# Routing operands moved from SBUF to PSUM in a one-core attention, expert and MLP kernel

## The chip, the cores and the metric

The kernel runs on one core of a Trainium2 chip. The metric is the device time of one execution in microseconds (us). The kernel before takes 499.25 us, the median of three runs (498.87 to 499.83). Besides these there is one profiled execution, from which all the rows below come.

## The reference

Three stages follow one another: attention over 2 batches and 8 heads with rotary positions, a top-1 mixture of 8 experts over 1152 tokens, and a dense MLP with a softplus-tanh gate. What matters here is the middle one: each token goes to the expert of its largest logit, so the kernel has to count the tokens of each expert and find a place for every token before any expert work can start.

```python
q_rot, k_rot = rotate(q), rotate(k)                  # 2 x 8 heads, 576 rows, 64 wide
scores = scale * q_rot @ k_rot.T
attn = exp(scores - max) / (sum + 1e-9);  x = attn @ v       # -> [1152, 512]
logits = x @ w_gate + modality_bias[modality_id]      # 8 experts
e_idx = argmax(logits);  gate_w = softmax(logits)[e_idx]
for e in range(8):
    mask = e_idx == e
    out[mask] = gate_w[mask] * (relu(x[mask] @ w1[e]) @ w2[e])
h = out @ w_in                                        # 512 -> 2048
g = h * tanh(softplus(h));  return g @ w_out
```

## The kernel before

The tokens are handled as two halves of 576, one for each batch. Products are made in float32 accuracy from pairs: each operand is split into a high part (`hi`, written by ScalarE) and a low part (`lo` = value minus `hi`, written by VectorE or GpSimd), and TensorE multiplies hi with hi, hi with lo and lo with hi.

Attention runs head by head. The order of its instructions on each engine is worked out ahead of time by a planner (`Plan`), which holds a modelled duration for each operation and always issues the one that can start first. While it works on the second half, the routing of half 0 is one of the planner's streams. The line `plan.op("rt_cp", "dve", 0.9, ...)` tells it how long the first block of VectorE operations behind the counting matmul takes, and `rest()` adds the following ones.

`routing(b)` is the routing of one half. From the logits it makes a one-hot table `oh`, lets TensorE count it by two matmuls into a PSUM bank `ps` (named `counts` for half 0 and `mm` for half 1), and makes from it each token's row number (`pos`, then `row` as int32, L405). GpSimd scatters the tokens' rows to DRAM with five indirect DMAs. Then comes a table of tiles: from the counts per expert (`ce`, `n1`, `qi`) the expert and first row of each tile of 304 tokens (`te`, `tm`, `tbl`). The helper `near` lays a small tile into a corner of a PSUM bank (`cur["rtile"]`, named `rt` or `sc` in the profile) in place of SBUF. `nx` is the number of tiles beyond the first two. `merge_extra` joins the leftover tiles of both halves into one list for a loop that runs only if there are any; its first line (L535) compares `iotat` (0, 1, 2, ...) with `nxs[0]`, half 0's count. With `mm`, `md` and `ei` it makes the list, and `nxi` is the sum of both counts.

The routing of half 1 runs after attention, beside the first expert tile. A loop at the end of the kernel goes through its steps, and after each VectorE step lets the generator of expert work (`gen0`) issue some TensorE work:

```python
for i, y in enumerate(chain(route(1), merge_extra(nx))):
    if i in P["dl"]:
        dec_load(len(wr))
    if y[0] == "dve":
        pump(P["rq"][(i > 9) + (i > 20)])
```

So VectorE's queue alternates between routing operations and the `hl` operations (L731) of the expert tile, which give TensorE the low part of its second product. An expert tile takes eight chunks of weights, `whi` (ScalarE, L609) and `wlo` (L614, GpSimd but for two chunks of the first tile). TensorE reads `hh`, `hl`, `whi` and `wlo` in its order (L706). Each engine takes its instructions strictly in the order issued. There are four expert tiles, (0, 0) to (1, 1). In between, VectorE decodes the weights of the last stage (`rt`, `wc`: L1318, L1323, L1328), a step after a set number of TensorE steps. The last stage is a loop over 2 groups and 16 blocks, whose costliest VectorE operation is a reciprocal (L1524).

Of the kernel before, what the change touches and what calls it, by code (L numbers as in the profile page):

```python
# [10 lines left out]
F32 = mybir.dt.float32  # L11
F32R = mybir.dt.float32r
I32 = mybir.dt.int32
AF = mybir.ActivationFunctionType
ALU = mybir.AluOpType
# [3 lines left out]
B, H, S, D = 2, 8, 576, 64  # L19
# [6 lines left out]
T = 304  # L26
# [186 lines left out]
def moe_kernel(ctx: ExitStack, tc: tile.TileContext, aps, out):  # L213
    nc = tc.nc
# [8 lines left out]
    rp = xctx.enter_context(tc.tile_pool(name="rp", bufs=1, side="right"))  # L223
# [16 lines left out]
    iotat = kp.tile([128, NS[1]], F32, name="iotat")  # L240
# [71 lines left out]
    scat, nxs, tes, tms = ([], []), [], [], []  # L312
    early = []

    def routing(b, bank):
        t = lambda sh, nm, dt=F32: rp.tile(sh, dt, tag=nm, name=f"{nm}{b}")
        side = True
        room = [0]

        def near(sh, nm):  # L320


            if not side:
                return t(sh, nm)
            n = 1
            for x in sh[1:]:
                n *= x
            o = room[0]
            room[0] += n
            v = cur["rtile"][0:sh[0], o:o + n]  # L330
            if len(sh) == 3:
                v = v.rearrange("p (a b) -> p a b", b=sh[2])
            return v

        V = nc.vector
# [4 lines left out]
            out=lg, in_=heads(X[b])[:, :, :, D:XW].rearrange("p j h e -> p j e h"),  # L340
# [15 lines left out]
            out=val, in0=lg, scalar=0.0, in1=iota8[:, 0:1, :].to_broadcast(sh),  # L356
            op0=ALU.is_ge, op1=ALU.mult,
# [9 lines left out]
        n = NE * 5  # L367
        yield "pe", 0.43, True
        ps = bank()
# [5 lines left out]
        def scan():  # L375
# [8 lines left out]
            out=base[:, 1:], data0=ps[:, 0:n], data1=zero[:, :n],  # L384
# [3 lines left out]
        V.tensor_tensor(out=pz, in0=ps[:, n:2 * n], in1=base[:, 0:n], op=ALU.add)  # L388
        V.tensor_copy(cnt[:, 0:n], ps[:, 0:n])
        V.tensor_tensor(out=pz, in0=pz, in1=ohf, op=ALU.mult)  # L390
        pos = t([128, 5], "pos") if b == 0 else near([128, 5], "pos")
        V.tensor_reduce(
            out=pos, in_=pz.rearrange("p (e j) -> p j e", j=5), axis=AX.X, op=ALU.add
        )
        sm8 = t([128, 5], "sm8")
        yield "dve", 0.12, True
        V.tensor_reduce(out=sm8, in_=ex, axis=AX.X, op=ALU.add)
# [1 line left out]
        nc.scalar.activation(out=sm8, in_=sm8, func=AF.Copy, bias=1e-9)  # L399
        yield "dve", 0.12, True  # L400
        V.reciprocal(out=X[b][:, :, XC + 1], in_=sm8)
        row = t([128, 5], "row", I32)
        s1, o1 = (-1.0, T + S - 1.0) if b == 0 else (1.0, float(T + S))
        yield "dve", 0.12, True
        V.tensor_scalar(out=row, in0=pos, scalar1=s1, scalar2=o1, op0=ALU.mult, op1=ALU.add)  # L405

        def scatters():
            for j, (_, qn) in enumerate(QT):
# [15 lines left out]
        else:  # L424
            cur["scatters"] = scatters()
            yield "mark", 0.0, False
            side = False
# [5 lines left out]
        n0 = t([1, NE], "n1")  # L433
# [5 lines left out]
            out=n1, in0=ce, scalar=float(T), in1=n0, op0=ALU.is_gt, op1=ALU.add  # L439
        )  # L440
        if side:
# [5 lines left out]
            out=qi, data0=n1, data1=zero[0:1, :NE], initial=0.0, op0=ALU.add, op1=ALU.add  # L447
# [7 lines left out]
            out=st, in0=s0, scalar=float(-T), in1=base[0:1, 0:n:5], op0=ALU.mult, op1=ALU.add  # L455
        )
        ns = NS[b]
        nx = t([1, 1], f"nx{b}")
        yield "dve", 0.12, True
        V.tensor_scalar(  # L460
            out=nx, in0=qi[:, NE - 1:NE], scalar1=-2.0, scalar2=None, op0=ALU.add
        )
        tv = iotat[0:1, 0:ns]
        if b:
# [3 lines left out]
                out=tv[:, 0:2], in0=iotat[0:1, 0:2], scalar1=nx, scalar2=None, op0=ALU.add  # L468
# [3 lines left out]
                out=tv[:, 2:ns], in0=iotat[0:1, 2:ns], scalar1=nxs[0], scalar2=-2.0,  # L472
                op0=ALU.subtract, op1=ALU.add,
# [7 lines left out]
            out=lt, in0=qi[:, None, :].to_broadcast(s8),  # L481
            in1=tv[:, :, None].to_broadcast(s8), op=ALU.is_le,
        )
        te = t([1, ns, 2], f"te{b}")
        tm = near([1, ns, 2], "tm") if side else te
        yield "dve", 0.12, True
        V.tensor_reduce(out=tm[:, :, 0], in_=lt, axis=AX.X, op=ALU.add)
        e8 = near([1, ns], "e8")
# [4 lines left out]
            out=lt, in0=iota8[0:1, 0:1, :].to_broadcast(s8),  # L493
            in1=e8[:, :, None].to_broadcast(s8), op=ALU.is_equal,
# [8 lines left out]
            out=cs, in0=tv, scalar=float(T), in1=cs, op0=ALU.mult, op1=ALU.add  # L503
# [9 lines left out]
            op0=ALU.max, op1=ALU.min,  # L513
# [2 lines left out]
        V.tensor_scalar(  # L516
            out=tm[:, :, 0], in0=tm[:, :, 0], scalar1=float(NE - 1), scalar2=None, op0=ALU.min
        )
        if side:
            yield "dve", 0.12, True  # L520
            V.tensor_copy(te, tm)
        tes.append(te)
        tms.append(tm)
        tbl[b] = ti = const.tile([1, 2, 2], I32, name=f"tbl{b}")
# [3 lines left out]
    def merge_extra(nx):  # L528

        V = nc.vector  # L530
        n0, n1 = NS[0] - 2, NS[1] - 2
        sh = [1, n0, 2]
        m = rp.tile([1, n0], F32, tag="mm", name="mm")
        yield "dve", 0.12, True
        V.tensor_scalar(  # L535
            out=m, in0=iotat[0:1, 0:n0], scalar1=nxs[0], scalar2=None, op0=ALU.is_lt
        )
        d = rp.tile(sh, F32, tag="md", name="md")
        yield "dve", 0.12, True
        V.tensor_tensor(out=d, in0=tes[0][:, 2:], in1=tms[1][:, 2:2 + n0], op=ALU.subtract)  # L540
        yield "dve", 0.12, True
        V.tensor_tensor(out=d, in0=d, in1=m[:, :, None].to_broadcast(sh), op=ALU.mult)
        yield "dve", 0.12, True
        V.tensor_tensor(
            out=tes[1][:, 2:2 + n0], in0=tms[1][:, 2:2 + n0], in1=d, op=ALU.add
        )
        ei = const.tile([1, n1, 2], I32, name="ei")
        yield "dve", 0.12, True
        V.tensor_copy(ei, tes[1][:, 2:])
        yield "dve", 0.12, True  # L550
        V.tensor_tensor(out=nx, in0=nxs[0], in1=nxs[1], op=ALU.add)
        cur["ei"] = ei

    def tile_regs(row):
# [676 lines left out]
    def hook(plan, bank):  # L1231

        r0 = route(0)
        cur["rbank"] = lambda: bank("counts")

        def until_mark():
            for y in r0:
                if y[0] == "mark":
                    return
                yield y  # L1240

        def mark(name):
            return lambda t: plan.done.update({name: ("dve", t)})

        def start():
            plan.add(until_pe(r0), plan.now, end=mark("rt"), gate=cur["spare"])

        def rest():
            next(r0)
            plan.add(until_mark(), plan.now + 0.8, end=mark("rt_row"))  # L1250

        def scatter():
            plan.add(cur["scatters"], plan.now, low=("pool",), end=mark("rt_sc"))

        def table():
            plan.add(r0, plan.now, end=mark("rt_end"))

        def weights():
            tile_rows(0)
            plan.add(until_pe(gen0), plan.now + 2.2, low=LOW)  # L1260

        z = 10.0 * H
        plan.op(
            "route", "sp", 0.0, z, start,
            deps=[("norm", n, f) for n in range(H) for f in range(2)],
        )
        plan.op("rt_mm", "pe", 0.43, z, lambda: next(r0), deps=["rt"], take=[("ring", "rt")])
        plan.op("rt_cp", "dve", 0.9, z, rest, deps=["rt_mm"], give=[("ring", "rt")])
        plan.op("scatter", "sp", 0.0, z, scatter, deps=["rt_row"])
        plan.op("table", "sp", 0.0, z, table, deps=["rt_row", ("plo", B * H - 1)])  # L1270
        plan.op(
            "rows", "sp", 2.2, z, weights,
            deps=["rt_end", "rt_sc", ("stack", B * H - 1), ("vload", B * H - 1)],
        )
# [430 lines left out]
```

## Time and profile before

| What | Value |
|---|---|
| Median of three runs | 499.25 us (498.87 to 499.83) |
| The profiled execution's own time | 501.34 us |
| Its span, first to last instruction | 499.5 us |
| TensorE busy, share of the span | 470.3 us, 94% |
| VectorE busy, share of the span | 399.8 us, 80% |
| GpSimd busy, share of the span | 361.1 us, 72% |
| ScalarE busy, share of the span | 332.8 us, 67% |
| Mean granted TensorE clock | 0.997 |

Engines are named as in the profile: PE is TensorE, DVE VectorE, ACT ScalarE, POOL GpSimd, SP the engine that only issues transfers. A row of the timeline gives start and duration in us, then engine, line, operation, written tile, read tiles and their shapes; behind it, in brackets, how long the engine had been idle and what it had waited for. A duration on VectorE can hold a wait that no bracket shows, since the instruction has already begun. The clock is given as a share of 2.4 GHz, so that 0.5 is 1.2 GHz.

### The profile page before, as it was taken

How to read it: one execution, taken by the hardware profiler on the slowest of the kernel's cores; microseconds unless marked ns; L12 is line 12 of the kernel's file. 1: busy time of each engine (PE TensorE's matmuls, PEld its weight loads, DVE VectorE, ACT ScalarE, POOL GpSimd, SP SyncE). 2: the span in 40 equal slices, each digit the busy share in tenths (PEclk: the TensorE clock that was granted, in tenths of full speed). 3: DMA queues.
4: the chain of work that ended last, by engine and by line, in shares of the span. 5: the costliest groups of instructions: out<-in, count | busy, mean ns of one | idle time of the engine just before them, and what ended most of it. 6: DMA issues, size and time to landing. Idle time of an engine off the chain costs nothing.

```text
span 499.5 us, 8770 instructions
## 1 busy us (share of the span) xinstructions
PE 470.3 (94%) x2996; PEld 430.3 (86%) x2996; DVE 399.8 (80%) x614; ACT 332.8 (67%) x751; POOL 361.1 (72%) x363
## 2 busy tenths in 40 slices
PE   1699999998999898999999999999999999999995
PEld 1589999997998797998999998898989887888894
DVE  5789889899798587663777779999999959777773
ACT  2488788777778754464564478666656778777663
POOL 3899989999870554675957457778678668977654
PEclk9999999999999998999999999999999999999999
DMA  6589985788564497786975340020200001100002
GB/s 218 137 200 240 227 232 149 183 214 193 150 175 142 160 394 283 259 309 249 326 283 211 113 141 0 2 85 1 85 1 1 1 1 42 42 22 1 1 0 86
DMA packets 24131, 69.41 MB, mean 139 GB/s; under 512 B 5522, under 2 KB 9810, under 8 KB 22034
## 3 DMA queue, kind: packets, MB, share of 16 engines
q1 hardware_dynamic: 21794, 63.16, 41.2%
q0 software_dynamic: 1456, 5.03, 2.5%
q10 hardware_dynamic: 832, 0.61, 0.4%
q8 instruction: 25, 0.41, 0.3%
q14 instruction: 24, 0.20, 0.1%
HBM read 49.08 MB, written 6.44 MB: 111 GB/s over the span
## 4 chain that ended last, share of the span: by engine, by line
PE 40%; DVE 8%; issue 3%; POOL 1%; ACT 1%; POOLq 0%; DVEq 0%; ACTq 0%
PE h L1498 15%; PE o L1559 14%; PE mm L706 11%; DVE ta L1524 6%; DVE wc L1328 1%; DVE ta L1525 1%; PE mm L672 0%; POOL out_dram L1569 0%; DVE wc L1318 0%; DVE wc L1323 0%; POOLq L1701 0%; POOL g L1542 0%; DVE idi L1645 0%; ACT ot L1565 0%; DVE yl L1436 0%
## 5 line engine op out<-in xcount | busy, mean ns | idle before, releaser
L1524 DVE RECIPROCAL ta<-ta 128x320 f32<-128x320 f32 (+1 forms) x64 | 124.6, 1947 | 21.4 <-ACT ta L1517 21.4
L1472 POOL TENSOR_TENSOR w2l<-wc,w2h 128x512 fp32r<-128x512 f32 x64 | 89.4, 1418 | 15.3 <-DVE yl L1436 8.1
L1559 PE MATMUL o<-w2h,g 128*128 128x512 f32 x288 | 97.8, 395 | 0.1
L1542 POOL TENSOR_TENSOR g<-ta,g 128x320 fp32r<-128x320 f32 (+1 forms) x63 | 52.9, 845 | 27.9 <-ACT g L1536 21.2
L969 PE MATMUL sc<-sk,sq 128*128 128x288 f32 (+1 forms) x320 | 58.3, 314 | 15.5 <-ACT sk L901 10.1
L1498 PE MATMUL h<-yl,w2h 128*128 128x320 f32 (+2 forms) x204 | 66.9, 328 | 0.1
L1498 PE MATMUL h<-yh,w2h 128*128 128x320 f32 (+2 forms) x204 | 66.9, 328 | 0.0
L1498 PE MATMUL h<-yh,w2l 128*128 128x320 f32 (+2 forms) x204 | 66.8, 328 | 0.0
L1559 PEld LDWEIGHTS o<-w2h,g 128*128 128x128 f32 x288 | 53.9, 188 | 12.2 <-POOL g L1542 1.0
L990 ACT ACTIVATE pexp<-sc,nm 128x576 f32<-128x576 f32 x72 | 53.3, 741 | 16.3 <-DVE nm L979 11.5
L1023 ACT ACTIVATE ph<-pt 128x512 fp32r<-128x512 f32 (+2 forms) x112 | 54.6, 509 | 12.5 <-PE pt L1003 12.0
L979 DVE TENSOR_REDUCE nm<-sc 128x1 f32<-128x576 f32 x72 | 53.4, 751 | 10.8 <-PE sc L969 7.3
L969 PEld LDWEIGHTS sc<-sk,sq 128*128 128x128 f32 (+1 forms) x320 | 46.4, 190 | 17.5 <-ACT sk L901 10.1
L1003 PE MATMUL pt<-ident,pexp 128*128 128x128 f32 (+1 forms) x360 | 54.9, 278 | 2.8 <-DVE pl L1029 1.7
L1559 PE MATMUL o<-w2l,g 128*128 128x512 f32 x144 | 56.8, 394 | 0.0
L1029 DVE TENSOR_TENSOR pl<-pt,ph 128x512 fp32r<-128x512 f32 (+1 forms) x80 | 48.9, 628 | 2.9 <-ACT ph L1023 2.4
L1044 PE MATMUL av<-ph,vhl 128*128 128x256 f32 (+1 forms) x160 | 50.8, 333 | 0.3 <-ACT avt L1053 0.2
L1003 PEld LDWEIGHTS pt<-ident,pexp 128*128 128x128 f32 (+1 forms) x360 | 42.1, 138 | 6.0 <-issue 2.1
L1536 ACT ACTIVATE g<-ta 128x320 fp32r<-128x320 f32 (+1 forms) x64 | 27.9, 435 | 22.5 <-DVE ta L1525 22.2
L1513 ACT ACTIVATE ta<-h 128x320 f32<-128x320 f32 (+1 forms) x64 | 25.6, 400 | 25.4 <-PE h L1498 25.3
L1498 PEld LDWEIGHTS h<-yl,w2h 128*128 128x128 f32 x204 | 38.3, 188 | 4.1 <-DVE yl L1436 0.4
L1498 PEld LDWEIGHTS h<-yh,w2h 128*128 128x128 f32 x204 | 38.3, 188 | 3.9 <-DVE ta L1525 0.2
(447 smaller groups left out, 1222.2 us busy)
## 6 DMA issues: line engine op xcount, KB each, us to landing
wr<-in_wio_dram SPq DMA_DIRECT2D x16, 1024.0 KB, 6.1
wc<-in_w_dram SPq DMA_DIRECT2D x26, 512.0 KB, 5.1
xs<-in_qk_dram SPq DMA_DIRECT2D x15, 576.0 KB, 5.3
sk<-ab SPq DMA_DIRECT2D x30, 288.0 KB, 4.1
sq<-ab SPq DMA_DIRECT2D x30, 144.0 KB, 2.7
vraw<-in_v_dram SPq DMA_DIRECT2D x16, 160.0 KB, 3.9
scratch<-zero SPq DMA_DIRECT2D x12, 108.8 KB, 4.5
xrow(0, 0)_2304<-scratch SPq DMA_DIRECT2D x2, 290.0 KB, 3.0
```

Of the source, the lines that this page charges most:

```text
L706: nc.tensor.matmul(ps[:, :T], lhsT=w, rhs=m, start=(n == 0), stop=(n == 3 * len(pairs) - 1))
L969: nc.tensor.matmul(t[:m, hf, :NC2], lhsT=sq[:, c:c + m], rhs=sk[:, z, hf * NC2:(hf + 1) * NC2], start=(z == 0), stop=(z == 1),)
L979: nc.vector.tensor_reduce(out=nm[n, j], in_=sc[n, j][:, :, :NC2], axis=AX.XY, op=ALU.max, negate=True)
L990: nc.scalar.activation(out=pe, in_=sc.pop((n, j))[:, :, :NC2], func=AF.Exp, bias=nm.pop((n, j)), accum_out=st[n, hf][:, i:i + 1],)
L1003: nc.tensor.transpose(out=t[:kn, o:o + 128], in_=pexp[n, j][:, k0:k0 + kn], identity=ident)
L1023: nc.scalar.activation(out=block(ph, n, hf, kts, slice(0, kn)), in_=psum(n, hf, kts, kn), func=AF.Copy)
L1044: nc.tensor.matmul(av[n, hf][:, :u.nq], lhsT=vhl[n][:, kt].rearrange("p a d -> p (a d)"), rhs=src[:, kt, u.at:u.at + u.nq], start=(kt == 0 ...
L1472: nc.gpsimd.tensor_tensor(out=lo[:, cs], in0=w[:, cs], in1=hi[:, cs].bitcast(F32), op=ALU.subtract)
L1498: nc.tensor.matmul(ps[:, :w], lhsT=wt[:, c], rhs=m[y][:, c], start=(n == 0), stop=(n == 11))
L1524: nc.vector.reciprocal(out=ta, in_=ta)
L1542: eng.tensor_tensor(out=gt[q][1][:, o:o + w], in0=tas.pop((q, i))[:, :w], in1=gt[q][0][:, o:o + w].bitcast(F32), op=ALU.subtract,)
L1559: nc.tensor.matmul(acc[g, t], lhsT=a[:, s], rhs=b, start=(f == 0 and z == 0), stop=(f == FC2 - 1 and z == 2),)
```

## The change

Three things are changed. The row numbers' sum `pos` goes into the counting matmul's own PSUM bank, and `row` is made from it at once, a few operations earlier than before (both halves). In `merge_extra` ScalarE first copies half 0's count from SBUF to PSUM (`first`), and the comparison becomes a TENSOR_TENSOR of `iotat` with that, written to PSUM. The merged list of half 1 is worked on in PSUM (`tm`), without the copy to `te` in SBUF. Two modelled durations of the planner are raised by 0.2.

```diff
-        pos = t([128, 5], "pos") if b == 0 else near([128, 5], "pos")
+        pos = ps[:, 3 * n:3 * n + 5]
         V.tensor_reduce(
             out=pos, in_=pz.rearrange("p (e j) -> p j e", j=5), axis=AX.X, op=ALU.add
         )
+        row = t([128, 5], "row", I32)
+        s1, o1 = (-1.0, T + S - 1.0) if b == 0 else (1.0, float(T + S))
+        V.tensor_scalar(out=row, in0=pos, scalar1=s1, scalar2=o1, op0=ALU.mult, op1=ALU.add)
...
         V.reciprocal(out=X[b][:, :, XC + 1], in_=sm8)
-        row = t([128, 5], "row", I32)
-        s1, o1 = (-1.0, T + S - 1.0) if b == 0 else (1.0, float(T + S))
-        yield "dve", 0.12, True
-        V.tensor_scalar(out=row, in0=pos, scalar1=s1, scalar2=o1, op0=ALU.mult, op1=ALU.add)
...
-        te = t([1, ns, 2], f"te{b}")
-        tm = near([1, ns, 2], "tm") if side else te
+        tm = te = near([1, ns, 2], "tm") if side else t([1, ns, 2], f"te{b}")
...
-        if side:
-            yield "dve", 0.12, True
-            V.tensor_copy(te, tm)
...
-        m = rp.tile([1, n0], F32, tag="mm", name="mm")
-        yield "dve", 0.12, True
-        V.tensor_scalar(
-            out=m, in0=iotat[0:1, 0:n0], scalar1=nxs[0], scalar2=None, op0=ALU.is_lt
+        o = cur["rtile"][0:1, 440:441 + n0]
+        first, m = o[:, n0:], o[:, 0:n0]
+        yield "act", 0.13, True
+        nc.scalar.activation(out=first, in_=nxs[0], func=AF.Copy)
+        yield "dve", 0.12, True
+        V.tensor_tensor(
+            out=m, in0=iotat[0:1, 0:n0], in1=first.to_broadcast([1, n0]), op=ALU.is_lt
         )
         d = rp.tile(sh, F32, tag="md", name="md")
+        t0 = tms[1][:, 2:2 + n0]
         yield "dve", 0.12, True
-        V.tensor_tensor(out=d, in0=tes[0][:, 2:], in1=tms[1][:, 2:2 + n0], op=ALU.subtract)
+        V.tensor_tensor(out=d, in0=tes[0][:, 2:], in1=t0, op=ALU.subtract)
...
-        V.tensor_tensor(
-            out=tes[1][:, 2:2 + n0], in0=tms[1][:, 2:2 + n0], in1=d, op=ALU.add
-        )
+        V.tensor_tensor(out=t0, in0=t0, in1=d, op=ALU.add)
...
-        V.tensor_copy(ei, tes[1][:, 2:])
+        V.tensor_copy(ei, tms[1][:, 2:])
         yield "dve", 0.12, True
-        V.tensor_tensor(out=nx, in0=nxs[0], in1=nxs[1], op=ALU.add)
+        V.tensor_tensor(out=nx, in0=first, in1=nxs[1], op=ALU.add)
...
-            plan.add(until_mark(), plan.now + 0.8, end=mark("rt_row"))
+            plan.add(until_mark(), plan.now + 1.0, end=mark("rt_row"))
...
-        plan.op("rt_cp", "dve", 0.9, z, rest, deps=["rt_mm"], give=[("ring", "rt")])
+        plan.op("rt_cp", "dve", 1.1, z, rest, deps=["rt_mm"], give=[("ring", "rt")])
```

VectorE's queue at the end of half 1's routing, before the change:

```order
L521 COPY te_2723<-rt_2545 1x36
L526 CAST tbl_2765<-rt_2545 1x4
L535 TENSOR_SCALAR mm<-iotat,nx_2116 1x8
L731 SCALAR_TENSOR_TENSOR hl(0, 0)_2576<-mm_2755,hh(0, 0)_2575 128x304
L540 TENSOR_TENSOR md<-te_2133,rt_2545 1x16
L542 TENSOR_TENSOR md<-md,mm 1x16
L544 TENSOR_TENSOR te_2723<-rt_2545,md 1x16
L549 CAST ei<-te_2723 1x32
L551 TENSOR_TENSOR nxi<-nx_2116,nx_2708 1x1
L731 SCALAR_TENSOR_TENSOR hl(0, 0)_2576<-mm_2779,hh(0, 0)_2575 128x304
```

The same place after the change (line numbers shift by a few; `rt` is the PSUM corner):

```order
L521 CAST tbl_2758<-rt_2544 1x4
L533 TENSOR_TENSOR rt_2544<-iotat,rt_2544 1x8
L539 TENSOR_TENSOR md<-te_2155,rt_2544 1x16
L541 TENSOR_TENSOR md<-md,rt_2544 1x16
L728 SCALAR_TENSOR_TENSOR hl(0, 0)_2575<-mm_2754,hh(0, 0)_2574 128x304
L543 TENSOR_TENSOR rt_2544<-rt_2544,md 1x16
L546 CAST ei<-rt_2544 1x32
L548 TENSOR_TENSOR nxi<-rt_2544,nx_2705 1x1
L728 SCALAR_TENSOR_TENSOR hl(0, 0)_2575<-mm_2781,hh(0, 0)_2574 128x304
```

The copy to `te` is gone, the comparison reads and writes `rt`, and two small operations stand ahead of the seventh `hl` that stood behind it.

ScalarE's queue there after the change; its new first-count copy is the second row:

```order
L606 ACTIVATE whi(0, 0)_5_2748<-wc_2537 128x1024
L531 ACTIVATE rt_2544<-nx_2124 1x1
L726 ACTIVATE hh(0, 0)_2574<-mm_2754 128x304
L726 ACTIVATE hh(0, 0)_2574<-mm_2781 128x304
L606 ACTIVATE whi(0, 0)_6_2798<-wc_2532 128x1024
```

Everything else in these rows stands as it did; the copy lies between the split of chunk 5 and the `hh` that the seventh `hl` reads.

VectorE's queue behind the counting matmul of half 0, inside attention, before the change:

```order
L392 TENSOR_REDUCE pos_1652<-counts 128x5
L397 TENSOR_REDUCE sm_1654<-ex_1510 128x5
L1029 TENSOR_TENSOR pl_1_1616<-pt_1_0_1603,ph_1_1615 128x512
L401 RECIPROCAL X_80<-sm_1654 128x5
L979 TENSOR_REDUCE nm_2_1687<-sc_111 128x1
L405 TENSOR_SCALAR row_1686<-pos_1652 128x5
L1084 TENSOR_TENSOR X_81<-xo_0_1636,rs_0_1479 128x3x72
L979 TENSOR_REDUCE nm_0_1702<-sc_110 128x1
L1068 RECIPROCAL rs_1_1618<-rs_1_1618 128x2
L1084 TENSOR_TENSOR X_81<-xo_1_1696,rs_1_1592 128x2x72
L1029 TENSOR_TENSOR pl_1_1616<-pt_1_2_1690,ph_1_1615 128x512
```

And after the change:

```order
L392 TENSOR_REDUCE counts<-counts 128x5
L397 TENSOR_SCALAR row_1653<-counts 128x5
L400 TENSOR_REDUCE sm_1655<-ex_1510 128x5
L1026 TENSOR_TENSOR pl_1_1616<-pt_1_0_1603,ph_1_1615 128x512
L404 RECIPROCAL X_80<-sm_1655 128x5
L976 TENSOR_REDUCE nm_2_1688<-sc_111 128x1
L1081 TENSOR_TENSOR X_81<-xo_0_1636,rs_0_1479 128x3x72
L976 TENSOR_REDUCE nm_0_1704<-sc_110 128x1
L1026 TENSOR_TENSOR pl_1_1616<-pt_1_2_1690,ph_1_1615 128x512
L1065 RECIPROCAL rs_1_1618<-rs_1_1618 128x2
L1081 TENSOR_TENSOR X_81<-xo_1_1695,rs_1_1592 128x2x72
```

The operation that makes `row` reads PSUM and stands four places earlier, and from here to the end of half 0's tile table the planner places a number of attention operations of all engines otherwise.

## Rows read from the trace of the kernel before

**Rows 1.** The chain of waits: start, duration, what; two long pieces.

```profile
235.59 20.28 PE mm L706 x144
257.95 33.60 PE mm L706 x240
```

**Rows 2.** Busy time by window: length, engines (instructions), PE clock, DMA share, GB/s.

```profile
100.00:120.00 20.00, 18.36 (x147) 17.59 (x147) 19.08 (x47) 14.86 (x40) 18.93 (x20) 1.00 0.80 211
...
188.00:190.00 2.00, 0.87 (x7) 0.61 (x5) 2.00 (x1) 1.46 (x3) 2.00 (x2) 1.00 1.06 440
190.00:192.00 2.00, 0.80 (x4) 0.54 (x4) 1.90 (x9) 0.00 (x0) 0.32 (x1) 1.00 0.99 411
192.00:194.00 2.00, 2.00 (x10) 2.00 (x11) 1.90 (x4) 1.37 (x2) 0.07 (x1) 0.59 0.96 373
194.00:196.00 2.00, 2.00 (x10) 2.00 (x10) 1.32 (x2) 0.00 (x0) 2.00 (x1) 0.55 0.35 135
```

**Rows 3.** TensorE's waits: for what, us in total, times, longest.

```profile
PE mm L706 <- DVE hl(0, 0)_2576 L731: 2.3, 2, 1.9
PE pt L1003 <- DVE pl L1029: 1.7, 3, 0.9
```

**Rows 4.** Timeline, VectorE and then GpSimd, 185 to 191 us.

```profile
186.24 0.18 DVE L521 COPY te<-rt 1x36 f32<-1x36 f32 x1
186.42 3.93 DVE L535 TENSOR_SCALAR mm<-iotat,nx 1x8 f32<-1x8 f32 x1
190.27 0.45 DVE L731 SCALAR_TENSOR_TENSOR hl(0, 0)_2576<-mm,hh(0, 0)_2575 128x304 fp32r<-128x304 f32 x1
...
185.59 2.42 POOL L614 TENSOR_TENSOR wlo(0, 0)_5_2751<-wc,whi(0, 0)_5_2749 128x1024 fp32r<-128x1024 f32 x1
187.97 2.35 POOL L614 TENSOR_TENSOR wlo(0, 0)_6_2803<-wc,whi(0, 0)_6_2801 128x1024 fp32r<-128x1024 f32 x1
```

**Rows 5.** Timeline of VectorE and GpSimd around 114 us.

```profile
113.84 1.69 DVE L405 TENSOR_SCALAR row<-pos 128x5 int32<-128x5 f32 x1
115.44 0.37 DVE L1084 TENSOR_TENSOR X<-xo,rs 128x216 f32<-128x216 f32 x1
...
112.84 2.66 POOL L912 TENSOR_TENSOR xs<-xs,tabs 128x1152 f32<-128x1152 f32 x1
```

**Rows 6.** Timeline of TensorE, 186 to 196 us, four of its matmuls.

```profile
186.05 0.30 PE L706 MATMUL mm<-hh(0, 0)_2575,whi(0, 0)_4_2697 128*128 128x304 f32 x1
...
188.56 0.30 PE L706 MATMUL mm<-hh(0, 0)_2575,whi(0, 0)_4_2697 128*128 128x304 f32 x1
190.78 0.41 PE L706 MATMUL mm<-hl(0, 0)_2576,whi(0, 0)_4_2697 128*128 128x304 f32 x1 [1.91 <-DVE hl(0, 0)_2576 L731]
...
195.91 0.30 PE L706 MATMUL mm<-hh(0, 0)_2575,whi(0, 0)_5_2749 128*128 128x304 f32 x1
```

**Rows 7.** Timeline of VectorE, GpSimd and ScalarE, 172 to 177 us.

```profile
173.95 0.22 DVE L365 TENSOR_TENSOR oh<-iota,rt 128x40 f32<-128x40 f32 x1
...
172.65 2.36 POOL L614 TENSOR_TENSOR wlo(0, 0)_2_2584<-wraw(0, 0)_2_2456,whi(0, 0)_2_2582 128x1024 fp32r<-128x1024 f32 x1 [3.36 <-ACT whi(0, 0)_2_2582 L609]
...
176.23 0.21 ACT L399 ACTIVATE sm<-sm 128x5 f32<-128x5 f32 x1 [2.70 <-DVE sm L397]
```

**Rows 8.** Timeline of TensorE, 115 to 118 us, the two rows with a wait.

```profile
115.95 0.38 PE L1003 MATMUL pt<-ident,pexp 128*64 128x128 f32 x2 [0.84 <-DVE X L1084]
...
117.49 0.84 PE L1003 MATMUL pt<-ident,pexp 128*128 128x128 f32 x6 [0.62 <-DVE pl L1029]
```

**Rows 9.** Timeline of VectorE at 182 us.

```profile
182.56 0.40 DVE L467 TENSOR_SCALAR tv<-iotat,nx 1x2 f32<-1x2 f32 x1
```

**Rows 10.** Timeline of SyncE and ScalarE for the first weight chunk of tile (0, 0).

```profile
154.93 0.34 SPq L602 DMA_DIRECT2D wraw(0, 0)_0_2332<-in_w_dram  x1
...
163.07 1.06 ACT L609 ACTIVATE whi(0, 0)_0_2345<-wraw(0, 0)_0_2332 128x1024 fp32r<-128x1024 f32 x1
```

**Rows 11.** DMA issues: KB each, median us from issue to landing.

```profile
wraw(0, 0)_0_2332<-in_w_dram SPq DMA_DIRECT2D x1, 512.0 KB, 4.4
```

## The prediction, made before the changed kernel was run

> **What bounds the kernel now.** I read the chain of waits first. From 235.6 us it runs through TensorE's L706 without a break, the two longest pieces among them 20 and 34 us long [rows 1], and goes on with TensorE and VectorE by turns to the end. So what TensorE loses before 235 us is lost at the end, unless another engine takes it back. The busy time by window shows where it loses: 1.64 us in the 20 us in which half 0's routing lies, and 1.13 and 1.20 us in the 4 us at the end of half 1's routing, with the clock at 0.59 and 0.55 in the 4 us behind that [rows 2]. TensorE's waits name the releasers: `hl` (L731) with 2.3 us in two waits, `pl` (L1029) with 1.7 us in three [rows 3]. The timeline of VectorE then shows what made them late. At 186.42 us L535, a TENSOR_SCALAR on eight numbers, takes 3.93 us; the copy ahead of it, on 36 numbers, takes 0.18 [rows 4]. GpSimd's two weight splits stand beside it without a gap, the second from 187.97 to 190.32 us, and L535 ends at 190.35 [rows 4]. Inside attention it is the same in small: L405 (`row`) takes 1.69 us and ends at 115.53, and GpSimd's product L912 ends at 115.50 [rows 5]. Both read SBUF and write SBUF. The copy at 186.24, PSUM to SBUF, ran beside the same split without delay [rows 4].
>
> **Half 1: the comparison.** L535 stands ahead of the seventh `hl` on VectorE, which therefore starts at 190.27 [rows 4], and TensorE, which wanted it after the matmul at 188.56, goes on at 190.78 [rows 6]. What this costs is read from the starts of the matmuls. From 186.05 to 188.56 there are 18 steps in 2.51 us, or 0.139 us a step. From 188.56 to 195.91 there are 21 steps in 7.35 us, where 21 x 0.139 = 2.93 would do [rows 6]. The loss is 4.42 us. It holds both waits (2.3 us, [rows 3]), the stretch at 0.59 and 0.55 of the clock, where 4 us x (1 - 0.57) = 1.7 us are lost [rows 2], and some 0.4 us of filling up again behind the waits.
>
> The new comparison is a TENSOR_TENSOR with `iotat` from SBUF, the count from PSUM, the result in PSUM. The trace has its like: L365 compares `iota` from SBUF with `rt` from PSUM and takes 0.22 us at 173.95, beside a GpSimd split that runs from 172.65 to 175.01 [rows 7]. I take 0.2 us for L533; from above it is bounded by L535's 3.93. The other operations of the list read one operand from SBUF and one from PSUM in the same way. Behind the new comparison the seventh and eighth `hl` come at some 187 us, and TensorE wants the seventh only behind 188.56. So the stall goes whole, and with it the 1.9 us wait that stands ahead of the slow clock: minus 4.4 us. What would be late next is `wlo` of chunk 6, which ends at 190.32 [rows 4]. TensorE then reaches chunk 5 at 186.05 + 24 x 0.139 = 189.4 us and chunk 6 not before 192.7 us, so it isn't.
>
> The added wait is that of L533 on ScalarE's copy of the count. Behind L533 on VectorE are two list operations and the seventh `hl`, and TensorE waits for that. The copy is a small ScalarE operation like L399 (0.21 us, [rows 7]), and reads a number that half 0's routing left long before; it stands behind the split of chunk 5, which must be over before GpSimd's own part of that chunk starts at 185.59 [rows 4]. VectorE gets to L533 at 186.3 or so. I cost it at nothing; if that cover were gone, every microsecond past some 188 us would come back to TensorE. The removed copy to `te` (0.18 us, [rows 4]) and its place in the loop, which issued two matmuls' worth of TensorE work, change the order of TensorE's work by nothing but where a register load stands. `row` of half 1 moves forward in the queue, but the scatters behind it also need the reciprocal's gate, which stays where it was.
>
> **Half 0: the row numbers.** L405's 1.69 us become some 0.2 us, since it now reads PSUM as the copy at 186.24 does [rows 4]: 1.5 us of VectorE time. Right behind it L1084 came at 115.44 [rows 5], for which TensorE had waited 0.84 us, and then 0.62 us for `pl` behind that [rows 8]. With VectorE 1.5 us earlier both waits go, which is 1.46 us at most. The other end is worked out from what else moves: the planner sets up to 40 us of attention in another order, and in the old one a misplaced `pl` costs up to 0.9 us [rows 3]; two such new waits would leave 1.46 - 2 x 0.9 = -0.3, a loss of 0.3 us. VectorE is 19.08 of 20 us busy there [rows 2] and a new order has no reason to be better or worse, so I stay near the row with the two waits and take minus 1.0 us. The two raised durations cost nothing by themselves; they only make the planner's order.
>
> **The sum.** 4.4 + 1.0 = 5.4 us off the profiled execution's own 501.34 us, 1.84 us of which lie outside its span of 499.5, gives 495.9 us. The median of the runs shown is 499.25, 2.1 us below the profiled one, and the same 5.4 us off it gives **493.8 us**. From 196 us to the last stage everything is set off by TensorE's progress, VectorE's decoding too, so I let the gain go through to the end.
>
> The Trainium skill, page "SBUF — State Buffer", section "Who interferes with whom", says that GpSimd's only pair of SBUF ports is VectorE's second pair, that it is held as an exclusive lock for a whole instruction, and that `copy`, `cast` and `tensor_scalar` from SBUF to SBUF, or an operation with two inputs in SBUF, are the ones that take it. By that rule the trace agrees: L535 and L405 both end 0.03 us behind a GpSimd operation [rows 4, 5]. The rule would leave the sum as it is, but it also speaks against the change, for the two `tv` operations ahead of the list stay TENSOR_SCALARs in SBUF; what that would do is the second rival.
>
> **Rivals.**
> *Half 1 alone pays.* The new order of attention eats what L405 gives back. For it: VectorE has little room there, and the waits of [rows 3] show that one late operation is enough. Against it: the two waits of [rows 8] stand right behind L405. Half 0 then comes to between +0.3 and -0.5, and the time is 499.25 - 4.4 + 0 = about 494.9, from 494.3 to 495.2.
> *The stall only moves.* The `tv` operations (L467 and the next) stay as they were. Before, the first ran at 182.56 in 0.40 us [rows 9], 3.0 us ahead of the first split at 185.59 [rows 4]. If they came later than that they would be held as L535 was, to the end of the second split, and TensorE with them: nothing is won in half 1, and 499.25 - 1.0 = 498.2. Against it: in the new queue they stand no later, behind the same `hl` and the same weight split. By the Trainium skill's page named above the same follows.
> *Other work takes a part back.* With TensorE 4 us further on, a weight chunk or a split comes late somewhere, or the clock falls in another place; the price of one such fall is the 1.7 us of [rows 2]. That makes 493.8 + 1.7 = 495.5, up to 497. Against it: the transfers' share falls to 0.35 at 194 us [rows 2], so they have room.
> *Slower: the tile table comes late.* Half 0's table is placed later by a few operations among attention's. SyncE needs it for the rows and issues the first weight chunk of tile (0, 0) behind it, at 154.93 us [rows 10]; it lands some 4.4 us later [rows 11], at 159.4, and ScalarE reads it at 163.07 [rows 10]. That leaves 3.7 us. From there on each microsecond of delay reaches the first expert tile, and to end above 500.3 the table would have to come 3.7 + 5.4 + 1.0 = 10 us late. A few operations of 0.7 us don't make that.
>
> **Chances and range.** About 0.2%, or 1.0 us, is what a measurement of this kernel can tell from no change. I give 0.60 to the forecast (493.8; by itself 492.8 to 494.4, the lower end if other waits of [rows 3] go too), 0.20 to half 1 alone (494.9), 0.12 to a part given back (495.5), 0.05 to a stall that moves (498.2, within reach of no change) and 0.03 to the late table. Faster by over 0.2% are the first three, and a little of the fourth: 0.92. Within: 0.05. Slower: 0.03. The range that should hold the time 8 times in 10 goes from 492.6, where half 0's two waits go whole and 0.8 us of the other waits of [rows 3] with them, to 496.4, where half of the loss behind the slow clock and all of half 0's gain are given back: 494.9 + 1.5.
>
> **What would show it.** In the changed profile the comparison, now L533, should take some 0.2 us, TensorE should go through chunks 4 and 5 of tile (0, 0) at 0.139 us a step without a wait for `hl`, and the clock should stay at 1.00 between 186 and 196 us. `row` of half 0 should take 0.2 us, and TensorE's busy time in the 20 us from 100 should rise from 18.36 towards 19.8. The prediction is wrong if a TENSOR_SCALAR of `tv` takes 2 us or more, if TensorE waits as long for something else in that tile, or if its first matmul of tile (1, 0), at 235.59 before, comes less than 4 us earlier.

## The result and the profile after

The changed kernel takes 493.63 us, the median of four runs (492.69 to 494.61); the kernel before, run beside it, takes 499.06 us (497.56 to 499.83). The ratio is 0.9895, with a 95% interval from 0.9865 to 0.9925. The profiled execution of after took 493.69 us with a span of 491.9 us, that of before 501.34 and 499.5. So the two traces differ by 7.6 us where the medians differ by 5.4: the profiled execution of before was 2.1 us above its median. Distances to before's trace below are therefore a little too large, and the medians say how large the effect is. Four profiles of the experiments lie off their medians as well: `cmp_early` by 2.2 and `cost_13` by 1.6 us above, `cmp_nx_back` by 1.2 and `half0_only` by 0.9 us below.

The chain of waits of after, beside [rows 1] (start, duration, what):

```profile
228.39 20.29 PE mm L703 x144
250.76 33.62 PE mm L703 x240
```

The same two pieces with the same lengths, 7.20 us earlier. From the first of them to the end of the span it is 263.5 us, and 263.9 before: what was won ahead of tile (1, 0) went through to the end.

To see where it was won, both traces are read from one common matmul, the first of attention that waits for `mx` (L347), to the first expert matmul of tile (0, 0) and on to the first of tile (1, 0). TensorE of after, three rows of its timeline:

```profile
100.10 0.40 PE L966 MATMUL sc<-sk,sq 128*128 128x288 f32 x1 [0.19 <-DVE mx L347]
...
168.36 0.41 PE L703 MATMUL mm<-xh(0, 0)_2503,whi(0, 0)_0_2368 128*128 128x304 f32 x1
...
228.39 0.38 PE L703 MATMUL mm<-xh(1, 0)_3275,whi(1, 0)_0_3302 128*128 128x304 f32 x1 [0.30 <-PEq L1407]
```

And of before, where the third row is the start in [rows 1]:

```profile
100.69 0.53 PE L969 MATMUL sc<-sk,sq 128*128 128x288 f32 x2 [0.18 <-DVE mx L347]
...
171.09 0.41 PE L706 MATMUL mm<-xh(0, 0)_2504,whi(0, 0)_0_2345 128*128 128x304 f32 x1
```

The stretch with half 0's routing in it went from 171.09 - 100.69 = 70.40 us to 68.26 (2.14 less), the stretch with half 1's from 235.59 - 171.09 = 64.50 to 60.03 (4.47 less). The other 0.59 us lie ahead of the common matmul, where nothing was changed. These two stretches are used for all the experiments.

**Half 1.** VectorE and then GpSimd of after, where [rows 4] stood:

```profile
183.23 0.15 DVE L521 CAST tbl<-rt 1x4 int32<-1x4 f32 x1
183.61 0.16 DVE L533 TENSOR_TENSOR rt<-iotat,rt 1x8 f32<-1x8 f32 x1 [0.23 <-issue]
183.80 0.16 DVE L539 TENSOR_TENSOR md<-te,rt 1x16 f32<-1x16 f32 x1
183.99 0.16 DVE L541 TENSOR_TENSOR md<-md,rt 1x16 f32<-1x16 f32 x1
184.52 0.47 DVE L728 SCALAR_TENSOR_TENSOR hl(0, 0)_2575<-mm,hh(0, 0)_2574 128x304 fp32r<-128x304 f32 x1 [0.36 <-ACT hh(0, 0)_2574 L726]
...
183.00 2.40 POOL L611 TENSOR_TENSOR wlo(0, 0)_5_2750<-wc,whi(0, 0)_5_2748 128x1024 fp32r<-128x1024 f32 x1
185.82 2.41 POOL L611 TENSOR_TENSOR wlo(0, 0)_6_2800<-wc,whi(0, 0)_6_2798 128x1024 fp32r<-128x1024 f32 x1 [0.42 <-ACT whi(0, 0)_6_2798 L606]
```

The comparison takes 0.16 us in the middle of `wlo` of chunk 5, and the seventh `hl` waits for nothing but its own `hh`. TensorE, for [rows 6]:

```profile
186.09 0.30 PE L703 MATMUL mm<-hh(0, 0)_2574,wlo(0, 0)_4_2699 128*128 128x304 f32 x1
...
189.84 0.31 PE L703 MATMUL mm<-hh(0, 0)_2574,wlo(0, 0)_5_2750 128*128 128x304 f32 x1
189.99 2.24 PE L669 MATMUL mm<-ident,xrow(0, 1)_2643 128*128 128x128 f32 x12
192.16 0.41 PE L703 MATMUL mm<-hh(0, 0)_2574,whi(0, 0)_6_2798 128*128 128x304 f32 x1
```

Between the first two rows lie 27 steps in 3.75 us, 0.139 us each, and no row in between has a wait.

**Half 0.** VectorE and TensorE of after, for [rows 5, 8], and by window for [rows 2]:

```profile
111.77 0.16 DVE L397 TENSOR_SCALAR row<-counts 128x5 int32<-128x5 f32 x1
...
113.28 0.38 DVE L1081 TENSOR_TENSOR X<-xo,rs 128x216 f32<-128x216 f32 x1
...
115.02 0.79 PE L966 MATMUL sc<-sk,sq 128*128 128x288 f32 x4 [0.28 <-ACT pexp L987]
...
146.09 0.89 PE L1071 MATMUL xo<-mov,avt 128*128 128x72 f32 x6 [0.63 <-DVE pl L1026]
148.96 0.27 PE L1000 MATMUL pt<-ident,pexp 128*64 128x128 f32 x1 [0.95 <-DVE tbl L521]
```

```profile
100.00:120.00 20.00, 19.62 (x158) 19.25 (x159) 19.08 (x50) 16.02 (x44) 18.68 (x23) 1.00 0.74 194
...
190.00:194.00 4.00, 4.00 (x27) 3.11 (x25) 2.75 (x7) 3.06 (x6) 1.57 (x2) 1.00 0.92 336
192.00:196.00 4.00, 4.00 (x29) 3.95 (x29) 3.71 (x7) 1.71 (x4) 2.28 (x1) 1.00 0.97 359
```

`row` takes 0.16 us, the two waits at 115 and 117 us are gone, TensorE is busy 19.62 of the 20 us for 18.36, and the granted clock stays at 1.00 behind 190 us. But 30 us later two waits of 0.63 and 0.95 us stand in attention, where before has 0.15 us (at 148.90) and 0.89 us (at 151.70): 0.54 us of TensorE's gain are lost there.

### The profile page after: what moved, and what is told of

Same layout as the page of the kernel before. It is cut to its first block, busy times and chain, and to the rows that moved or that the text cites. A ratio compares the mean times of both kernels' runs of the same rounds, so it can differ in the third digit from the quotient of the medians.

```text
span 491.9 us, 8773 instructions
## 1 busy us (share of the span) xinstructions
PE 465.8 (95%) x2996; PEld 428.4 (87%) x2996; DVE 392.8 (80%) x613; ACT 333.6 (68%) x752; POOL 361.1 (73%) x363
## 4 chain that ended last, share of the span: by engine, by line
PE 51%; POOL 0%; issue 0%; ACT 0%; POOLq 0%; DVE 0%
PE h L1495 20%; PE o L1556 20%; PE mm L703 11%; PE mm L669 0%; POOL out_dram L1566 0%; POOLq L1698 0%; ACT ot L1562 0%; DVE yl L1433 0%; ACT yh L1431 0%; ACT Y L753 0%; POOL spacer L1573 0%; POOLq L1566 0%
## 5 line engine op out<-in xcount | busy, mean ns | idle before, releaser
L1469 POOL TENSOR_TENSOR w2l<-wc,w2h 128x512 fp32r<-128x512 f32 x64 | 90.4, 1433 | 16.4 <-ACT w2h L1468 8.3
L1539 POOL TENSOR_TENSOR g<-ta,g 128x320 fp32r<-128x320 f32 (+1 forms) x63 | 51.8, 827 | 27.6 <-ACT g L1533 21.0
L1495 PEld LDWEIGHTS h<-yh,w2l 128*128 128x128 f32 x204 | 38.4, 188 | 2.3
```

Of the source, the lines that this page charges most:

```text
L1469: nc.gpsimd.tensor_tensor(out=lo[:, cs], in0=w[:, cs], in1=hi[:, cs].bitcast(F32), op=ALU.subtract)
L1495: nc.tensor.matmul(ps[:, :w], lhsT=wt[:, c], rhs=m[y][:, c], start=(n == 0), stop=(n == 11))
L1539: eng.tensor_tensor(out=gt[q][1][:, o:o + w], in0=tas.pop((q, i))[:, :w], in1=gt[q][0][:, o:o + w].bitcast(F32), op=ALU.subtract,)
```

## Experiments

### The two parts apart

`half1_only` is the kernel before with the new `merge_extra` and the list in PSUM; `half0_only` is the kernel before with these lines alone. The first ones belong to both halves, so half 1's `row` moves too and its routing has one step less:

```diff
-        pos = t([128, 5], "pos") if b == 0 else near([128, 5], "pos")
+        pos = ps[:, 3 * n:3 * n + 5]
...
+        V.tensor_scalar(out=row, in0=pos, ...)    # moved up, behind the sum
...
-            plan.add(until_mark(), plan.now + 0.8, end=mark("rt_row"))
+            plan.add(until_mark(), plan.now + 1.0, end=mark("rt_row"))
...
-        plan.op("rt_cp", "dve", 0.9, ...)
+        plan.op("rt_cp", "dve", 1.1, ...)
```

Expected of `half1_only`: 

> The changed merge of half 1 alone (comparison and list in PSUM), half 0's row numbers as before. Theory: the two parts are independent, and half 1's is worth the 4.4 us read from the matmul starts of the kernel before: 499.06 - 4.4 = 494.7 us. The comparison takes 0.2 us, the clock stays at 1.00 from 180 to 200 us, and L405 of half 0 still takes 1.7 us. Rival: the gain in half 1 needs the other phase that half 0's new order gives it, then the gain here is under 3 us, over 496.

Expected of `half0_only`: 

> The row numbers in PSUM with the planner's two raised durations alone, the merge of half 1 as before. The prediction's term gives 499.06 - 1.0 = 498.1 us; the traces of before and after differ by 2.2 us between the same two waits of TensorE at 100 and at 149 us, which gives 496.9. The old comparison still takes about 3.9 us and the clock still falls behind it. Rival: half 0 gives nothing by itself (499.1).

Measured: `half1_only` 495.02 us, ratio 0.9925 [0.9904, 0.9945]; `half0_only` 497.22 us, ratio 0.9975 [0.9959, 0.9992]; the kernel before beside them 498.99. The product of the ratios is 0.9900, the whole change 0.9895: two gains that add up. The half 1 stretch of `half1_only` is 60.00 us, as in after. The gain of `half0_only` can't be put down to half 0 alone: its half 0 stretch is 68.52 us for 70.40 before, but its half 1 stretch is 62.79 us for 64.50 too, with the clock at 1.00 where before had 0.57. `half0_only` also showed what the comparison's price is made of. VectorE, GpSimd and TensorE:

```profile
183.28 2.00 DVE L533 TENSOR_SCALAR mm<-iotat,nx 1x8 f32<-1x8 f32 x1
185.21 0.15 DVE L538 TENSOR_TENSOR md<-te,rt 1x16 f32<-1x16 f32 x1
185.29 0.46 DVE L729 SCALAR_TENSOR_TENSOR hl(0, 0)_2575<-mm,hh(0, 0)_2574 128x304 fp32r<-128x304 f32 x1
185.67 2.31 DVE L540 TENSOR_TENSOR md<-md,mm 1x16 f32<-1x16 f32 x1
...
182.85 2.41 POOL L612 TENSOR_TENSOR wlo(0, 0)_5_2751<-wc,whi(0, 0)_5_2749 128x1024 fp32r<-128x1024 f32 x1
185.60 2.36 POOL L612 TENSOR_TENSOR wlo(0, 0)_6_2802<-wc,whi(0, 0)_6_2800 128x1024 fp32r<-128x1024 f32 x1 [0.35 <-ACT whi(0, 0)_6_2800 L607]
...
188.89 0.41 PE L704 MATMUL mm<-hl(0, 0)_2575,whi(0, 0)_4_2697 128*128 128x304 f32 x1 [2.40 <-DVE hl(0, 0)_2575 L729]
```

Here the comparison is held to the end of `wlo` 5 only, for 0.35 us lie between the splits; [rows 4] have no such gap, and there it was held across both. Then the product `md` times `mm`, two operands from SBUF, is held by `wlo` 6, and TensorE waits 2.40 us for the `hl` behind it. The comparison isn't the only operation that can be held.

### The comparison alone

`cmp_back` is the changed kernel with the old comparison; `cmp_early` is the kernel before with the comparison moved ahead of all of half 1's routing, where no split runs.

```diff
 cmp_back
-            out=m, in0=iotat[0:1, 0:n0], in1=first.to_broadcast([1, n0]), op=ALU.is_lt
+            out=m, in0=iotat[0:1, 0:n0], scalar1=nxs[0], scalar2=None, op0=ALU.is_lt
 cmp_early
+        nc.vector.tensor_scalar(out=cur["m"], in0=iotat[...], scalar1=nxs[0], ...)
         for i, y in enumerate(chain(route(1), merge_extra(nx))):
```

Expected of `cmp_back`: 

> The changed kernel with the one comparison as it was, a TENSOR_SCALAR from SBUF to SBUF, all else changed. Theory: this one operation is the whole of half 1's gain, so it takes over 3 us again, ending with a weight split of GpSimd, and the time is 493.6 + 4.4 = 498.0 us. Rival: the removed copy, the list in PSUM or the other order of the queue did it, then 493.6 to 494.5.

Expected of `cmp_early`: 

> The kernel before with the old comparison issued ahead of half 1's routing, at some 169 to 170 us, where GpSimd stands idle from 169.3 to 172.6; same operation, same operands. Theory: only the GpSimd work beside it makes it slow, so it takes 0.2 us there, and the time is 499.06 - 4.4 = 494.7 us without any operand in PSUM. Rival: an operation of this form is slow by itself, then it takes 3.9 us at its new place too and the time stays at 498 us or more.

Measured: `cmp_back` 495.10 us (0.9923 [0.9897, 0.9948]), `cmp_early` 496.66 us (0.9937 [0.9914, 0.9961]). Both expectations were missed: putting the comparison back costs 1.5 us by the medians, where 4.4 were expected, and taking it away gives 2.3. The five executions of `cmp_early` spread widely, from 494.94 to 498.88 us; two of them came within 0.3 us of the expected 494.7, and the profiled one is the slowest. VectorE and GpSimd of `cmp_back`:

```profile
184.06 2.12 DVE L534 TENSOR_SCALAR mm<-iotat,nx 1x8 f32<-1x8 f32 x1
186.10 0.15 DVE L540 TENSOR_TENSOR md<-te,rt 1x16 f32<-1x16 f32 x1
186.28 0.16 DVE L542 TENSOR_TENSOR md<-md,mm 1x16 f32<-1x16 f32 x1
...
183.72 2.42 POOL L612 TENSOR_TENSOR wlo(0, 0)_5_2750<-wc,whi(0, 0)_5_2748 128x1024 fp32r<-128x1024 f32 x1
186.49 2.40 POOL L612 TENSOR_TENSOR wlo(0, 0)_6_2801<-wc,whi(0, 0)_6_2799 128x1024 fp32r<-128x1024 f32 x1 [0.34 <-DVE md L542]
```

The comparison is held 2.12 us, and the product gets through the gap between the splits. Its half 1 stretch is 60.64 us, so one hold costs 0.6 us in the trace: TensorE still has matmuls ahead of the seventh `hl`. Where the rest of the 1.5 us lies is not shown. In the profile of `cmp_early` the comparison takes 0.2 us at its new place, and two other operations are held instead, the product `md` times `mm` and the last sum of the merge:

```profile
186.21 0.61 DVE L538 TENSOR_TENSOR md<-md,mm 1x16 f32<-1x16 f32 x1
...
187.14 2.36 DVE L547 TENSOR_TENSOR nxi<-nx,nx 1x1 int32<-1x1 f32 x1
...
184.36 2.42 POOL L610 TENSOR_TENSOR wlo(0, 0)_5_2753<-wc,whi(0, 0)_5_2751 128x1024 fp32r<-128x1024 f32 x1
187.12 2.37 POOL L610 TENSOR_TENSOR wlo(0, 0)_6_2803<-wc,whi(0, 0)_6_2801 128x1024 fp32r<-128x1024 f32 x1 [0.34 <-ACT whi(0, 0)_6_2801 L605]
```

```profile
188.00:192.00 4.00, 2.11 (x12) 2.06 (x12) 3.90 (x6) 2.24 (x4) 1.53 (x2) 0.86 1.02 421
192.00:196.00 4.00, 4.00 (x22) 3.66 (x20) 2.05 (x3) 0.62 (x2) 2.35 (x1) 0.71 0.58 200
```

The product is held by what was left of `wlo` 5, 0.61 us. The last sum, on one number, takes 2.36 us, to the end of `wlo` 6. TensorE waits 1.89 us for the eighth `hl`, the clock falls to 0.86 and 0.71, and the half 1 stretch is 63.69 us. What happened in the quicker executions is not known, since they left no profile.

So a second theory: every VectorE operation of this list that takes two operands from SBUF, and the TENSOR_SCALAR from SBUF to SBUF, is held to the end of the split it meets. One hold is nearly absorbed; the second makes the `hl` late.

### The second theory

`nx_back` is the changed kernel with the last sum back on two SBUF operands; `cmp_nx_back` has the old comparison too.

```diff
-        V.tensor_tensor(out=nx, in0=first, in1=nxs[1], op=ALU.add)
+        V.tensor_tensor(out=nx, in0=nxs[0], in1=nxs[1], op=ALU.add)
```

Expected of `nx_back`: 

> The changed kernel, with the last sum of the merge (nx) again of two SBUF operands. Theory (an operation with two SBUF operands is held to the end of the GpSimd split beside it, and to no later): in the changed kernel this sum comes at 185.21, and the split wlo_5 ends at 185.40, so it is held 0.2 us at most, gets out in the 0.42 us before wlo_6, and the time stays at 493.5 to 494.0. Rival (any such operation beside the two splits is held across both, or waits for wlo_6): 2 to 3 us held, the 8th hl that late, TensorE waits some 2 us, 496 to 497.

Expected of `cmp_nx_back`: 

> The changed kernel with both the comparison (TENSOR_SCALAR from SBUF to SBUF) and the last sum (two SBUF operands) put back. With the comparison alone back the time was 495.1, and there the last sum stood at 187.06, in the middle of the split wlo_6 (186.49 to 188.89). Theory (each such operation is held to the end of the split it meets, one hold is absorbed, the second isn't): comparison held 2.1 us, sum held 1.8 us, the 8th hl at about 189 for 187.13, TensorE waits about 2 us for it, 496.7 to 497.5. Rival (the comparison is the price, the sum adds its length alone): 495.0 to 495.5 and no wait for hl.

Measured: `nx_back` 493.57 us (0.9896 [0.9872, 0.9920]), `cmp_nx_back` 497.02 us (0.9962 [0.9944, 0.9980]). Both times are as the theory has it. VectorE and GpSimd of the second, and TensorE's wait:

```profile
182.94 2.11 DVE L534 TENSOR_SCALAR mm<-iotat,nx 1x8 f32<-1x8 f32 x1
...
185.93 2.01 DVE L549 TENSOR_TENSOR nxi<-nx,nx 1x1 int32<-1x1 f32 x1
...
182.62 2.40 POOL L612 TENSOR_TENSOR wlo(0, 0)_5_2750<-wc,whi(0, 0)_5_2748 128x1024 fp32r<-128x1024 f32 x1
185.57 2.37 POOL L612 TENSOR_TENSOR wlo(0, 0)_6_2801<-wc,whi(0, 0)_6_2799 128x1024 fp32r<-128x1024 f32 x1 [0.55 <-ACT whi(0, 0)_6_2799 L607]
```

```profile
PE mm L704 <- DVE hl(0, 0)_2575 L729: 1.9, 1, 1.9
```

The sum that cost nothing alone (0.15 us, at 185.19, just at the end of its split) is held 2.01 us once the comparison has pushed it beside `wlo` 6.

### Which operand holds

The changed kernel with the comparison in two other forms, its output in PSUM in both:

```diff
 cmp_out_psum
+            out=m, in0=iotat[0:1, 0:n0], scalar1=nxs[0], scalar2=None, op0=ALU.is_lt
 cmp_two_sbuf
+            out=m, in0=iotat[0:1, 0:n0], in1=nxs[0].to_broadcast([1, n0]), op=ALU.is_lt
```

Expected of `cmp_out_psum`: 

> The changed kernel with the comparison as TENSOR_SCALAR again, its inputs in SBUF, its output in PSUM; read is its duration alone, beside wlo_5. Theory (what is held needs SBUF on both sides, or two SBUF inputs): 0.15 to 0.25 us. Rival (SBUF inputs alone decide): held to the end of wlo_5, 1.8 to 2.2 us. The time of one look: 493 to 496.

Expected of `cmp_two_sbuf`: 

> The changed kernel with the comparison as TENSOR_TENSOR of two SBUF operands, output in PSUM; read is its duration alone, beside wlo_5. With one SBUF operand as TENSOR_SCALAR and the output in PSUM it took 0.22. Theory (two SBUF inputs are held wherever the output goes): 1.8 to 2.2 us, to the end of wlo_5. Rival (SBUF on both sides is what holds): 0.15 to 0.25 us. The time of one look: 493 to 496.

Measured, in one run each: 493.66 and 493.52 us. The comparison in `cmp_out_psum`, with its split behind it:

```profile
183.59 0.22 DVE L533 TENSOR_SCALAR rt<-iotat,nx 1x8 f32<-1x8 f32 x1 [0.23 <-issue]
...
182.97 2.40 POOL L611 TENSOR_TENSOR wlo(0, 0)_5_2750<-wc,whi(0, 0)_5_2748 128x1024 fp32r<-128x1024 f32 x1
```

And in `cmp_two_sbuf`:

```profile
182.72 1.81 DVE L533 TENSOR_TENSOR rt<-iotat,nx 1x8 f32<-1x8 f32 x1 [0.23 <-issue]
...
182.08 2.41 POOL L611 TENSOR_TENSOR wlo(0, 0)_5_2750<-wc,whi(0, 0)_5_2748 128x1024 fp32r<-128x1024 f32 x1
```

The TENSOR_SCALAR goes free when its output alone is in PSUM; the TENSOR_TENSOR with two operands from SBUF is held to 0.04 us behind the split in spite of it. That hold costs little here, as in `cmp_back`: the half 1 stretches are 60.03 and 60.76 us. The Trainium skill, page "SBUF — State Buffer", section "Who interferes with whom", says that an operation with two SBUF inputs contends with a GpSimd operation that reads SBUF, and a `tensor_scalar` only in the mode that takes both port pairs; these two runs agree, though no row names the mode.

### Half 0: the row or the list

Four kernels with the new half 1 part make a square: `row` late and from SBUF, or early and from PSUM; the planner's two costs at 0.9 and 0.8, or at 1.1 and 1.0. `half1_only` and the changed kernel are two corners. `old_plan` is the changed kernel with the old costs, `slow_row_new_plan` is `half1_only` with the new ones.

```diff
 old_plan
-        plan.op("rt_cp", "dve", 1.1, ...)
+        plan.op("rt_cp", "dve", 0.9, ...)
```

Expected of `old_plan`: 

> The changed kernel with the two planner costs of half 0's routing back at 0.9 and 0.8 (the list of the work between 107 and 150 us is the old one but for the row numbers). Theory (the quick row of half 0 gives its 2 us, the list nothing): 493.4 to 494.0, row 0.2 us, TensorE without the two waits at 115 and 117. Rival (the new list gives 1 us or more of it): 494.6 to 495.2, and the 2.2 us by which the attention stood earlier at 149 shrink to about 1.

Expected of `slow_row_new_plan`: 

> The merge part of the change, half 0's and half 1's routing as before (row numbers from SBUF to SBUF, late), but with the planner's two costs at 1.1 and 1.0. It completes the four cases: old row and old list 495.02, new row and old list 495.03, new row and new list 493.6. Theory A (the two need each other: the old row is held beside GpSimd's work in any list, so the new list gains nothing by itself): 494.7 to 495.4. Theory B (the list alone is worth 1.4 us, the quick row nothing): 493.4 to 494.0.

| `row`, list | Median, us | Before beside it, us | Ratio | Half 0 stretch, us |
|---|---|---|---|---|
| old, old (`half1_only`) | 495.02 | 498.99 | 0.9925 [0.9904, 0.9945] | 69.72 |
| new, old (`old_plan`) | 495.03 | 499.06 | 0.9919 [0.9902, 0.9936] | 69.45 |
| old, new (`slow_row_new_plan`) | 493.73 | 498.33 | 0.9907 [0.9885, 0.9929] | 69.10 |
| new, new (after) | 493.63 | 499.06 | 0.9895 [0.9865, 0.9925] | 68.26 |

The theory for `old_plan` fell: the quick row with the old list gains nothing that can be measured. It is as quick there as in after (0.16 us at 111.81), yet the wait for `pl` at 115 us stays in part, 0.40 us for 0.63 in `half1_only`, and the one at 150 us stays whole, 0.88 for 0.89:

```profile
115.69 0.85 PE L1000 MATMUL pt<-ident,pexp 128*128 128x128 f32 x6 [0.40 <-DVE pl L1026]
...
150.20 0.38 PE L1000 MATMUL pt<-ident,pexp 128*64 128x128 f32 x2 [0.88 <-DVE pl L1026]
```

`slow_row_new_plan`, whose `row` takes 1.66 us at 113.17, hit theory B's time, but the kernel before was 0.7 us quicker in that company, so its gain, 4.60 us, lies between 3.97 (`half1_only`) and 5.43 (after). The intervals overlap; the stretch, free of the start and of half 1, says 0.3 us for the row alone, 0.6 for the list alone, 1.5 for both. How well it repeats: seven profiles with the new row and the new list lie between 67.96 and 68.52 us, three of the old pair at 69.72, 69.80 and 70.40. So the stretches show that both together give 1.2 us or more; the split between row and list is only likely.

Two more lists: `cost_12` has the two costs at 1.2 and 1.1 us, `cost_13` at 1.3 and 1.0.

Expected of `cost_12`: 

> The changed kernel with that cost at 1.2 us, which moves few entries of the list (67 rows of TensorE's stand differently). Theory: within 0.5 us of the changed kernel, 493.2 to 494.2. Rival (each list is a new draw): 1 us or more away from it.

Expected of `cost_13`: 

> The changed kernel with the planner's cost of half 0's position chain at 1.3 us for 1.1, so that the list between 110 and 150 us is a third one. Theory (what the list brings is where the bursts happen to fall, not how true the cost is): anywhere from 493 to 495, another set of waits of TensorE from 115 to 150. Rival (the truer the cost the better; the chain runs from 110.54 to 111.93, 1.4 us, in the changed kernel): 493.0 to 493.5.

Measured: `cost_12` 492.88 us (0.9883 [0.9860, 0.9905]), `cost_13` 493.73 us (0.9900 [0.9882, 0.9918]); stretches 67.90 and 68.20 us. `cost_12` lies 0.3 us below its expected range, but the kernel before beside these two took 498.33 us: the gains are 5.45 us for `cost_12` and 4.60 for `cost_13`, against 5.43 for the changed kernel. Neither can be told from the changed kernel, and the larger cost, nearer to the measured chain, isn't the better one.

## Why the prediction was right, and where its steps weren't

*Half 1, minus 4.4.* The stretch lost 4.47 us, and `half1_only` gained 4.0 by its median. By the medians the term was thus some 0.4 us too large; it had been read from an execution 2.1 us above the median. What was predicted to show it did: the comparison at 0.16 us, the steps at 0.139, the clock at 1.00, and `tv` (L466, L470) at 0.22 us each, so the rival of a moved stall had no ground in this change. The wait for ScalarE's copy, costed at nothing, can be no more than the 0.23 us ahead of the comparison, and TensorE has no wait behind it. But the cause was put too narrowly. It named one operation; `cmp_early` took just that one away and left 496.66 by its median, and in its profile the product and `nxi` were held in its place. The change works because it leaves no operation of the merged list in a form that is held (two operands from SBUF, or a TENSOR_SCALAR from SBUF to SBUF), which the prediction had only in the half sentence that the other operations read SBUF and PSUM "in the same way". And the 3.93 us were a matter of phase: with a gap between the splits the same comparison takes 2.0 to 2.1 us, and by itself it lengthens the stretch by 0.6 us (`cmp_back`).

*The slow clock.* It was counted as part of the stall. In before and `cmp_early` it followed the wait; in `half0_only` and `cmp_nx_back` waits of 2.40 and 1.9 us passed with the clock at 1.00 in every 4 us stretch from 180 to 208. There the half 1 stretches are 62.79 and 62.55 us, against 64.50 and 63.69. Nor does a fall need such a stall: in `cost_13` the clock was 0.61 from 168 to 172 us, behind waits of TensorE (0.53 and 0.47 us) that stand in `cost_12` too, where it stayed at 1.00, and the half 1 stretch is 61.34 us for 60.05. What decides it stays open. The gain doesn't hang on it: eight executions of the kernel before had a mean clock of 0.999 or 1.000, and they took 497.07 to 498.95 us, where the slowest of the changed kernel took 494.61.

*Half 0, minus 1.0.* Mis-sized, and the failed step is "a new order has no reason to be better or worse" with "the two raised durations cost nothing by themselves". Both edits together gave 5.43 - 3.97 = 1.46 us by the medians, 1.5 by the stretch against `half1_only` (2.14 against before's own profile, whose `row` took 1.69 us, for 1.21 in `half1_only` with the same code). That equals the prediction's upper bound, but not for its reason: the quick row alone, which was to take both waits away, gave 0.3. Not settled is how the list does it. Counted from the common matmul, TensorE's idle time falls by 0.5 us from `half1_only` to after; the other 1.0 lies in what the profile counts as busy, in which the modelled ends of pipelined matmuls are contained.

*The sum and the range.* That 5.4 us forecast and 5.43 measured agree so closely is luck in part: half 1 was taken some 0.4 us too large and half 0 0.5 too small. The upper end of the range was added wrongly. Half of the 1.7 us behind the slow clock is 0.85, and with half 0's gain given back too that makes some 495.7, not 496.4; the result lies below both.

*The rest.* No part of the gain was given back in the bulk behind 228 us, and the tile table was not late.

## What to carry to other kernels

A tiny operation that takes microseconds beside another engine's long one is held; look at all its neighbours with the same operands before pricing it, because the next one takes the place of the first. What a hold costs is what is left of it when the consumer's queued work runs out: by the half 1 stretch the first 2 us cost 0.6 here (60.03 to 60.64 us, `cmp_back`), the second 2 us another 1.9 (62.55, `cmp_nx_back`). And when a change moves a planner's costs along with the code, test the two apart, since the reordered list may carry more than the code.

## What was not expected of the hardware

A TENSOR_TENSOR on one number, two operands from SBUF, took 2.36 us beside a GpSimd split, and an output in PSUM did not save the comparison with two operands from SBUF (1.81 us). A gap of 0.34 us between two splits was enough to let the product `md` times `mm`, with two operands from SBUF, through (`cmp_back`); without a gap one operation was held across both, 3.93 us. And a wait of TensorE of 2.40 us left the granted clock at 1.00, where one of 1.91 us in another kernel was followed by 0.57; each was seen in one execution.
